# The list of all steps put in another order: packed attention and SwiGLU MLP on one core

## The chip, the cores and the metric

The kernel runs on one core of one Trainium2 chip. The metric is the device time of one execution in microseconds (us), as the median of several runs; a lower time is better. The engines of the core are called PE (TensorE), ACT (ScalarE), DVE (VectorE), POOL (GpSimd) and SP (SyncE, which here only issues transfers).

## The reference

Two stages follow each other. The attention takes q, k and v of 8 batches, 8 heads, 576 tokens and 64 elements, and p of 8 batches, 8 heads, 32 rows and 64 elements. The MLP takes the attention's output as 4608 tokens of 512 elements.

```python
packed = sm_attn(p, k, v)          # 32 rows per batch and head
out = sm_attn(q, packed, packed)   # softmax(q @ packed.T / 8) @ packed
x = out.transpose(0, 2, 1, 3).reshape(4608, 512)
xn = x / sqrt(mean(x * x, axis=-1) + 1e-06) * rms_g
g = xn @ w_gate                    # 512 x 1536
val = xn @ w_val                   # 512 x 1536
result = (g * 1 / (1 + exp(-g))) * val @ w_out   # 1536 x 512
```

## The kernel before

The 4608 tokens are cut into 12 units of 384 tokens (NU = 12), and the attention into 8 batches. The first attention, of p on k and v, is called stage 1 in the code and done batch by batch; the second attention, of q on the packed rows, and the MLP are done unit by unit. The product of a batch's packed rows with the gate and value weights is computed ahead ("packed weights", kept in buffers named ring), and the MLP's first product of a unit runs on it.

Every strand of work is a Python generator, called a chain: the keys, the loads of v, stage 1, the loads and conversions of the weights, the gram steps (which take scales from the weights), the queries, the attention of the units, the packed weights of the batches, and the MLP. A chain yields a step at a time and says on which engine the step runs. Each step issues a few instructions. `Plan.run` (L107 to L128) goes through the list `ORDER` (L129 to L181), two letters for a step, takes for each entry the chain of that number and issues its next step. Since every engine executes its instructions in the order in which they were issued, the list fixes the order on PE, ACT, DVE and POOL and the order in which SP issues transfers. No engine overtakes; which engine waits for which follows from the data and from the rooms (buffers) that chains take and give back. The list has 3289 entries, of which 903 are steps on PE, 903 on ACT, 830 on DVE, 427 on POOL and 226 on SP. A wait ahead of a step holds up all later steps of the same engine.

`FILLS` (L182 to L185) lists matmuls on dummy data (256 columns each, L1826) with the number of the PE step ahead of which they are put, how many of them and into which buffer they write.

The lines that matter in what follows: the gram steps are matmuls at L467, L472 and L517, with DVE at L470 to L478 and POOL at L482 to L489. Weights are converted by POOL (L410), DVE (L412) and ACT (L406). The packed weights are matmuls at L1074 and L1086, evicted by ACT at L371 and by DVE at L373. Stage 1 has its scores at L774, POOL's sum of two halves at L884 (behind a DMA transpose, L879) and its values at L915. The attention of a unit has its scores at L1327, the softmax on DVE at L1341 to L1351, transposes on PE at L1201 with copies by ACT at L1211, the values at L1398, a power step on POOL at L1444, a scaling of the result e on ACT at L1476, and the copies of the transposed result by ACT at L1225 and DVE at L1227. The MLP's gate and value products are at L1527, its SiLU on ACT at L1609, the product with it on DVE at L1612, and its last product at L1592, with a variant of seven products at L1723 for the later units.

Of the kernel before, what the change touches and what calls it, by code (L numbers as in the profile page):

```python
# [44 lines left out]
class Plan:  # L45
# [89 lines left out]
    "A9A-AZAZAZAfAeAcBAA5A+AeAdBAAVAfBAA+A6AfA1AbA6AYA5A4A4A5BAA5A5A5A6BBAeAZAZAeAdA5AfAUA6AfBCBBA1AVA6BCAZA6A6BCAfBB"
    "A6AgAYBBAgAZBEAgBEAZAZBDBDArA5BCBDA1BFA6A5ArA6AsBFBDBEAZACAZA6ACBEArACAsACAtACBGACBGAZAXACBFACAXBGAZAZAZBFAsBGAC"
    "ACBHACBIAWACACAZAXAtAYBHBIACAXAtAAAAAAAAAAAAAvBIAuAWAABHAZAZAZAZAZAZBHAZAZAuAXAWAAAXAAAZAZAXAuAZAvAXAYAXAXAZAWAA"
    "AwAYAZAZAwBJAXAvAABJAABJAXBJAZAZBIAXAwAXAXAWAZAZAZAZAAAXAXAWAXAXAWAWAWAZAZAZAZAZAZAXAWAXAZBKBLAWAAAXAYAAAAAXAABM"
    "AXBMAXAAAZBMAAAXAABMAZAZAZAXAABLBKAZAXAAAZAZAZAZAZAZAXAABNAZBOAZAXAYBOBPBPAYBOAZAXBPBOAABRAXBQBQAXBQAABQBRAZAZAZ"
    "AYBPBSBRAABSAAAAAYAXAZBRBUBTBTBUBTBSAXBSBTBUAZAZAYBUAZAZAXBVBVAYAXBWAXAXBVBWBWAZAZBXBXAXBWBYAABXAYBVBYBXACBYACAY"  # L140
    "BaBaBaAXBYAZAZBbAXACAZAZBaBbACAZAXAZACBcACBcBbAZAZBbBcBdAXAXAWBdAWBcBZBZACBeAXAZAXAWAZAXBeAWBdAXAZAXACBdAXAXAZAC"
    "AWBeACACACAZAAAAAAACAWAAAWAZAABeAZAZAZAZAZBNAZAZAZAXAZAZAAAWAZAZAAAZACACACACACAZAZACAZAZAAAAAAAWAAAZAAAWACBfAZAZ"
    "AABgAAAABfAWACBgACACACACACAZAAAAACACACAZAZACAAAZACAAAYAAAZACAAAXAZAZAYAZACAXAZAZAZAABhACAAAhBhBiAhAAAYAXBhAYAZBk"
    "AXAZAZBkBjBlBkBlBkAhAZAZAZBmBlAYAZBjAABhBmAAAYAXAhBlBmBnAXBjBnAZAZBmBjAYBoBoBoAABnBpAhAYBqAABpBnAXBqBqAZAZAZBqBr"
    "BoAhBpBrAZAZBiAAAXBrBpAYBsBrAhAZAZBuBsAXAXBuBsAXAXBuAXAXAZAZBsACAhBvBtAZAZAhBvAZBuBwBvACBvBxACAYBwAXAhBxByAhAYAC"
    "ACAhByAXAXAZAZBxAYAhACAWBwB0B0AZAWAXAXBtAWBwB0BxAWAXAZAZB0AZAZAZAZAWAZACBzAXBzAXAXAXAXAXBzACAhAWAZAZACACACACBzAC"
    "ACAAAAAAAAAhAWAXAZAZAZB1AZACACACAZAZAZAZAZAZAZAZAZAAAhAZAWAZAZAZB1ACAAAWAAAWAhACAhAWACAhAWAAAAAAB2AhByAAAZACACAC"
    "AAAhAhACACAhAZAZAZAZAZACB2AAACACACACAhACACByAhAAAXAYB3AZAhAXB3AZAZAZAZACAAB4AXB3AZAXAhB5AYAZB5AhACB7B5AhB5B7AkAh"
    "B3AhAXB6AZAZAZAZB7B6AkB8AhB8B7B9AhB9B8AhAAB8AZAZAZAZB-AhAXAhB-AAB6AhB-B9B-B9AZAZAAAhACAhCAB6CAAXB+AACAACAAB+CAAX"
    "AZAZAXAXAZB+CBAACBAAB+AZAXCBCCAXAZAZAZAXAXAAAhAACCCBCCAZAXAXAhAXAhCCAhCECDCEAXAhAZAXAXCEAACEAhAXAAAZAAAZCDAZAZAX"  # L150
    "AWB4AAAZCDCFAWAhCFCFCDAhCFAAAXAXAhAZAZAZAZAZAZAZAZAZAZAZAZAZAZACAXAhAZAXAhAWAXAXAhAWAhAWAZAZAZCHAWAWAWAWAWAXAZAZ"
    "AhACAZACACACAZAZAZAZAZAZAWAhACAhAhAhAhAhCHAXACCGAhAhACAhAXCIAZAZAZAZAhACACAhACAhACACAXAXAZAACGAAAZAZAAAZACCKAXAA"
    "CJAZAZCICKCKCLAXAhCLAXAYAZCKCNCMAhCLACCMAZCNAhCMAZCJAXCNCLCOCMAAAZAhAZAZCOACAhAXAXCNAXAXAXAAACAAAXAYAXCOCPAZAXCP"
    "AhCOAXCQACCQCQAACRCQAhAYCRAACSAhCSCPAZAZAZAhCSCPAhCTAACSAAAhAAAhAhCTCRACAZAZAZAlAAAYCUCVCUCUCUAlCTCWCRCTCVCWAZAZ"
    "CWAAAACWACCXACAAAACXAZAlAlAZAZAAAZCZCVCYACAAAXCYAAAACVCXCZAZAZACAZAZCYAWAACZCYCXAZACAXACAAAZAZAhCZAZAZAlAXAAAXAC"
    "ACACACAWAWAWAXAZAZAZAZAWCaAZAXAZACAXAXAWACCaAWACAlAXAlAZAZAWAWACAWAAACAlAAAmAmAmAZAZAYCbAYCcAAAmAmAmCcCbAAAZCcCb"
    "AXAWAZAZCcCbAlAZAZACAlAZAZAZAZAZAZAmAXAZAZAACdAmAXAmAmAXACAZAZAZACAZACAZAnAnAnAnAnCdAnACAZCfAXCgAZAZChAkAZAZAXCg"
    "ACAZChCiAZAXCiAYCgAnCiCjAnCgCkAkAYCfCeClCkCjCkClCiAZAZCjClCkAoChAZAZAoCmChAZAXCnCmACCmAnClCnACAZAkAkCnAYCoAnCoAo"
    "AoCpCnAXCpAXCpCoAoAoCmCoAZAZAXAZACCqACCjCqAZAZCpAXAXAoAkAZCrCrAXCrAoAZAZCsAXCqCsCsCtAXCtACACACACAAAZAZAZCrAAAWAX"
    "AZCuAZAXACAAAZCsCqAZAZAAAAAWAAAAACCuAAApApApAYACCeACAAACAWAAAAAZCuAXAZCtACAWCvAAAACtAZAZAWAoCuAWAXAoAWAXAWAWAZAZ"  # L160
    "AZAZAZAZAXCwAWAXAWACCvACAXAZAZAZAZApACAAAAAAAACwAAAXAZAZACAXAACvAWCvAAAXAZACACAZAZAZAAAXAZAZAZAZAAACACApAAACApAC"
    "ApACACACApACAYAAApApAXCxCyCyAqAZAZAZAZAZAZCyACAqAqAqAqAqAXAZAZAACxCyAkAXAACzAAC0AXAXAZAZAYAZAAC1AqC0C0AZAZAXC2C1"
    "C0AqC2AZC3ACC1ACAqC1C3C4C2C1C1C1C1C3C2C4AACzACAqAZAZC6C1C4C1C1C1ACAZAZC6C4C1ACC6C3C1C7C7C6C4AXC4C4ACC4ACC7ACAZC7"
    "C7C7AZAZAZC9C4C7ACC9C8AXC8C9C7C4AXC9C8C4C8AXAZAZC-C7C7AXC-C-C7C9AZAZAZC9C-C7C4AXC9C9C5ACACC4C+AXAXC4AXAXC+AXC7C+"
# [24 lines left out]
)
# [1692 lines left out]
```

## Time and profile before

| what | value |
| --- | --- |
| runs | 715.92, 718.26, 715.59 us |
| median | 715.92 us |
| profiled execution | 717.6 us, with a span of 715.8 us |
| PE busy in the span | 697.8 us (97%) |
| DVE, ACT, POOL busy | 515.4, 496.2, 350.1 us |
| instructions of PE | 8367 matmuls and as many weight loads |
| mean granted clock | 0.998 of 2.4 GHz |

The span goes from the first to the last instruction of one execution; the rest of its time lies outside. PE counts as busy from a matmul's start to its end. The matmuls overlap, so a mean duration of one is longer than the time that it adds. Idle time in brackets behind an instruction is time in which its engine did nothing ahead of it, with what ended that wait. A line of ACT, DVE or POOL with a wait is of interest only where PE comes to wait for it.

### The profile page before, as it was taken

What the parts mean: (1) busy time and instruction counts of PE and PEld (TensorE: products, weight loads), DVE (VectorE), ACT (ScalarE), POOL (GpSimd) and SP (SyncE); (2) the same over time, 40 slices, a digit from 0 to 9 for tenths busy, and PEclk for the clock granted to TensorE, in tenths of its full rate; (3) what the DMA queues carried; (4) which work ended last, traced back from release to release, by engine and by line L of the source; (5) the groups of instructions that cost most, each with busy time, mean ns of one, the idle gap of its engine ahead of it and who ended that gap; (6) DMA issues with size and microseconds to landing.
All of it is one profiled execution on the core that took longest, in us unless ns stands there. A gap on an engine that the chain in (4) does not pass through costs nothing.

```text
span 715.8 us, 20438 instructions
## 1 busy us (share of the span) xinstructions
PE 697.8 (97%) x8367; PEld 460.4 (64%) x8367; DVE 515.4 (72%) x1126; ACT 496.2 (69%) x1095; POOL 350.1 (49%) x468
## 2 busy tenths in 40 slices
...
GB/s 294 367 375 260 239 3 83 104 164 167 50 166 186 253 136 209 210 115 145 247 225 210 183 113 248 162 224 234 186 138 192 124 164 64 148 104 38 31 0 45
DMA packets 157103, 118.23 MB, mean 165 GB/s; under 512 B 117201, under 2 KB 140497, under 8 KB 153170
## 3 DMA queue, kind: packets, MB, share of 16 engines
...
q8 instruction: 65, 1.06, 0.6%
...
## 4 chain that ended last, share of the span: by engine, by line
PE 81%; DMA 6%; DVE 4%; ACT 4%; POOL 3%; issue 2%; SPq 1%; POOLq 0%; ACTq 0%; DVEq 0%
PE pm_1x L1527 9%; PE pm_3x L1527 9%; PE pm_0x L1527 8%; PE pm_2x L1527 8%; PE pm_3x L1592 8%; PE pm_2x L1592 7%; PE pm_0x L1592 5%; PE pm_1x L1723 3%; PE pm_0x L1723 3%; PE pm_3x L1723 3%; PE pm_2x L1723 2%; DMA ring<-in_moe_w_gate_dram 2%; PE psa L1086 1%; PE psb L915 1%; PE psa L1327 1%
## 5 line engine op out<-in xcount | busy, mean ns | idle before, releaser
L1527 PEld LDWEIGHTS <-ring 128*128 128x128 f16 x2304 | 204.7, 98 | 86.5 <-issue 14.9
L1592 PEld LDWEIGHTS <-hall 128*128 128x128 f16 x792 | 74.9, 98 | 89.0 <-issue 4.0
L1656 POOL TENSOR_TENSOR hall<-a_0x,hall 128x384 f16<-128x384 f32 (+1 forms) x36 | 32.5, 903 | 64.9 <-ACT hall L1653 64.8
L1637 POOL TENSOR_TENSOR hall<-t_1x,hall 128x384 f16<-128x384 f32 x32 | 32.7, 1021 | 59.3 <-ACT hall L1634 52.0
L1592 PE MATMUL pm_2x<-wo,hall 128*128 128x512 f16 x252 | 57.3, 379 | 0.0
L1592 PE MATMUL pm_3x<-wo,hall 128*128 128x512 f16 x252 | 56.8, 379 | 0.0
L1592 PE MATMUL pm_0x<-wo,hall 128*128 128x512 f16 x216 | 48.3, 379 | 0.0
L1527 PE MATMUL pm_0x<-aTu_0x,ring 128*128 128x384 f16 (+1 forms) x318 | 45.8, 287 | 1.2 <-DVE t_1x L1612 0.8
L1527 PE MATMUL pm_1x<-aTu_1x,ring 128*128 128x192 f16 (+1 forms) x336 | 47.0, 283 | 0.0
L1723 PEld LDWEIGHTS <-hall 128*128 128x128 f16 x432 | 41.9, 98 | 5.9
L1527 PE MATMUL pm_3x<-aTu_1x,ring 128*128 128x384 f16 (+1 forms) x306 | 44.6, 288 | 0.1
L1527 PE MATMUL pm_1x<-aTu_0x,ring 128*128 128x384 f16 (+1 forms) x300 | 43.5, 288 | 0.3 <-DVE ring L373 0.2
L1159 POOL TENSOR_TENSOR wgv<-o_0x,wgv 128x512 f16<-128x512 f32 x19 | 22.9, 1203 | 34.9 <-ACT wgv L1157 34.9
L1527 PE MATMUL pm_3x<-aTu_0x,ring 128*128 128x192 f16 (+1 forms) x276 | 39.0, 284 | 0.4 <-ACT t_1x L1609 0.3
L1527 PE MATMUL pm_2x<-aTu_1x,ring 128*128 128x384 f16 (+1 forms) x258 | 37.7, 289 | 0.7 <-ACT t_1x L1609 0.7
L1527 PE MATMUL pm_2x<-aTu_0x,ring 128*128 128x384 f16 (+1 forms) x258 | 36.7, 285 | 0.3 <-ACT t_1x L1609 0.3
L1527 PE MATMUL pm_0x<-aTu_1x,ring 128*128 128x192 f16 (+1 forms) x252 | 35.5, 284 | 0.0
L1637 POOL TENSOR_TENSOR hall<-t_0x,hall 128x384 f16<-128x384 f32 x24 | 23.9, 997 | 19.7 <-ACT hall L1634 18.3
L884 POOL TENSOR_TENSOR a1T_0x<-a_1x 96x768 f32<-96x768 f16 x9 | 15.1, 1676 | 37.0 <-DMA a_1x<-hl_0x 25.4
L373 DVE SCALAR_TENSOR_TENSOR ring<-psa,ring 128x512 f16<-128x512 f32 x30 | 20.6, 686 | 11.5 <-ACT ring L371 11.5
L371 ACT ACTIVATE ring<-psa 128x512 f16<-128x512 f32 x30 | 17.8, 593 | 13.5 <-DVE ring L373 6.7
L1653 ACT CAST hall<-a_0x 128x384 f16<-128x384 f32 (+1 forms) x36 | 17.6, 488 | 9.0 <-DVE a_0x L1612 8.5
...
## 6 DMA issues: line engine op xcount, KB each, us to landing
...
```

The source lines that it names most:

```text
L371: nc.scalar.activation(hi, x, AF.Copy, scale=s)
L373: nc.vector.scalar_tensor_tensor(lo, x, s, hi, ALU.mult, ALU.subtract)
L884: nc.gpsimd.tensor_tensor(a1T, x[:, 0], x[:, 1], ALU.add)
L915: nc.tensor.matmul(pp[32 * j : 32 * j + 32, :D], a1T[:, c, 32 * j : 32 * j + 32], vf[:, j, cv, :], start=(c == 0), stop=(c == NCK - 1),)
L1086: nc.tensor.matmul(ps[e][32 * j : 32 * j + 32, :], pg[h, lp, j, :], w16[h, j, lw, :], start=(n3 == 0), stop=(n3 == 2),)
L1159: nc.gpsimd.tensor_tensor(wgv16[:, c, k, 1], st, wgv16[:, c, k, 0], ALU.subtract)
L1527: nc.tensor.matmul(psi[:, :, o : o + n], pw[:, g, lw, w, f * P : (f + 1) * P], aT[:, :, la, g, o : o + n], start=(j == 0), stop=(j == 5),)
L1592: nc.tensor.matmul(po, hall[:, ft, lh, ts], wo[:, ft, 1 - lw, :], start=(n == 0), stop=(n == 3 * NFT - 1))
L1637: nc.gpsimd.tensor_tensor(hall[:, ft, 1, :], t, hall[:, ft, 0, :], ALU.subtract)
L1653: nc.scalar.copy(h3[:, 0, own], x3[:, own])
L1656: nc.gpsimd.tensor_tensor(h3[:, 1, own], x3[:, own], h3[:, 0, own], ALU.subtract)
L1723: nc.tensor.matmul(ps[:, :q], A[k](c, la), W[k](c, lw), start=(c + n3 == 0), stop=(c == NFC - 1 and n3 == 2))
```

## The change

Only the list `ORDER` and the list `FILLS` change. All functions, all buffers and all instructions on the data stay. The new list has the same 3289 entries in another order. Of the steps of each engine this many stay at the same place of their engine's order: 665 of 903 on PE, 286 of 903 on ACT, 255 of 830 on DVE, 185 of 427 on POOL, 117 of 226 on SP. The lists are text of letters; their first and last lines and the fillers are these:

```diff
 ORDER = (
-    "ABAAAAAAAAAAADAAAWAEAFAAAAAAAAAAAAAAAAADAAAAAAAAAAAAABAxADAxAyADAxADAEAyAWAWAxAxAxAxAGAHAWAxAyAEAxAEAFAxAFAFAyAW"
...
-    "AZAZEYAZEYEYAZEWAZAZAZAZAZEaAZAZAZAZAZEaAZEaAZEZEaEZAZAZAZAZAZAZEaEaEaEaAZEaAZEaEa"
+    "ABAAAAAAAAADAAAAAAADAAAAAAAAAAAAAAAAAAAAAWADAAAAAAADAxAEAWAxAWAFAxAxAyAEAxAyAxABAxAWAxAyAEAWAEAxAWAFAGAHAIAJAyAD"
...
+    "AZAZEYAZAZAZEYEYEYAZAZAZEZEaAZAZAZAZAZAZEaAZEaAZAZEaAZAZAZAZAZAZEaAZEaEaEZEaEaEaEa"
 )
 FILLS = (
-    (0, 29, "pm", 0), (1, 4, "pm", 0), (8, 5, "pa", -1), (20, 3, "psc", 0), (23, 1, "psc", 0),
-    (24, 5, "psc", 0), (28, 37, "pm", 0), (31, 6, "pm", 0),
+    (0, 29, "pm", 0), (5, 4, "psc", 0), (20, 3, "psc", 0), (21, 2, "psc", 0), (23, 3, "psc", 0),
+    (25, 6, "pm", 0), (28, 16, "pa", -1), (29, 12, "pm", 0), (35, 8, "pm", 0), (41, 2, "psc", 0),
+    (42, 4, "psc", 0),
 )
```

## Rows read from the trace of the kernel before

**Rows 1.** Part 1 of the page: busy us, share, instructions of each engine.

```profile
PE 697.8 (97%) x8367; PEld 460.4 (64%) x8367; DVE 515.4 (72%) x1126; ACT 496.2 (69%) x1095; POOL 350.1 (49%) x468
```

**Rows 2.** Chain that ended last: start us, length us, what, instructions.

```profile
165.32 7.77 PE pm_0x L1592 x36
```

**Rows 3.** Stretches: length; busy PE, PEld, DVE, ACT, POOL; clock, DMA share, GB/s.

```profile
0.00:53.70 53.70, 45.92 (x663) 35.52 (x663) 36.69 (x80) 31.80 (x59) 28.25 (x47) 0.97 1.01 345
53.70:80.00 26.30, 24.29 (x246) 15.24 (x238) 23.99 (x41) 21.86 (x38) 19.35 (x23) 1.00 0.76 261
...
490.00:712.60 222.60, 222.41 (x2399) 156.78 (x2396) 129.81 (x284) 123.80 (x309) 109.42 (x186) 1.00 0.40 105
```

**Rows 4.** Timeline of PE: start us, length us, engine, instruction, [idle before, releaser].

```profile
310.77 0.39 PE L1086 MATMUL pm_3x<-wgv,pgh_0x 64*32 64x512 f16 x1
...
313.26 0.37 PE L1086 MATMUL pm_3x<-wgv,pgh_0x 64*32 64x512 f16 x1 [2.10 <-issue]
```

**Rows 5.** Timeline of PE near 465 us, stage-1 values of batch 6.

```profile
465.57 0.88 PE L915 MATMUL psb<-big_4x,a1T_0x 96*32 96x64 f32 x48 [0.76 <-DMA big_4x<-in_v_dram]
```

**Rows 6.** Part 3 of the page: DMA queue, packets, MB, share of 16 engines.

```profile
q8 instruction: 65, 1.06, 0.6%
```

**Rows 7.** Timeline of DVE in the front.

```profile
40.43 1.22 DVE L412 SCALAR_TENSOR_TENSOR wgv<-wgv,hall 128x1024 uint32<-128x1024 uint32 x1
...
52.54 0.94 DVE L1227 SCALAR_TENSOR_TENSOR aTu_0x<-psa,aTu_0x 128x768 f16<-128x768 f32 x1
```

**Rows 8.** Timeline of ACT in the front.

```profile
42.07 0.71 ACT L371 ACTIVATE ring<-pm_3x,gv_r 128x512 f16<-128x512 f32 x1
...
45.62 1.35 ACT L1476 ACTIVATE e_0x<-e_0x,trio_3x 128x256 f32<-128x256 f32 x3
```

**Rows 9.** Timeline of POOL in the front.

```profile
39.08 1.22 POOL L482 TENSOR_SCALAR tiny_14x<-tiny_14x 128x2 f32<-128x2 f32 x1
...
40.70 1.09 POOL L484 TENSOR_SCALAR ratio<-tiny_14x,gv_r 128x1 f32<-128x1 f32 x1
42.75 0.88 POOL L1444 TENSOR_TENSOR trio_2x<-trio_1x,neghalf 128x3 f32<-128x3 f32 x1 [0.96 <-DVE trio_1x L1438]
...
46.63 0.27 POOL L484 TENSOR_SCALAR ratio<-tiny_16x,gv_r 128x1 f32<-128x1 f32 x1
```

**Rows 10.** Timeline of PE, first and last wait between 53.7 and 80 us.

```profile
65.09 1.14 PE L1527 MATMUL pm_0x<-aTu_0x,ring 128*128 128x384 f16 x6 [0.77 <-DVE t_1x L1612]
...
78.01 1.14 PE L1527 MATMUL pm_0x<-aTu_0x,ring 128*128 128x384 f16 x6 [0.45 <-ACT a1T_0x L867]
```

**Rows 11.** Timeline of PE: two batches' stage-1 scores (L774) and values (L915).

```profile
207.01 0.67 PE L774 MATMUL psa<-big_1x,pT_0x 128*32 128x288 f16 x16
...
221.36 0.88 PE L915 MATMUL psb<-big_5x,a1T_0x 96*32 96x64 f32 x48
...
222.06 0.68 PE L774 MATMUL psa<-big_3x,pT_0x 128*32 128x288 f16 x16
...
234.08 0.88 PE L915 MATMUL psb<-big_4x,a1T_0x 96*32 96x64 f32 x48 [0.24 <-POOL a1T_0x L884]
```

**Rows 12.** Timeline of POOL, its sum of the first of these batches.

```profile
218.67 1.63 POOL L884 TENSOR_TENSOR a1T_0x<-a_0x 96x768 f32<-96x768 f16 x1 [1.19 <-DMA a_0x<-hl_0x]
```

**Rows 13.** Timeline of PE, attention of the second unit.

```profile
102.06 0.85 PE L1201 MATMUL psb<-ident,e_0x 128*128 128x128 f32 x6 [0.26 <-DVE e_0x L1351]
...
105.80 0.27 PE L1398 MATMUL psa<-pk_0x,aT_0x 32*64 32x64 f32 x1
```

**Rows 14.** Timeline of ACT, attention of the second unit.

```profile
103.18 0.57 ACT L1211 ACTIVATE aT_0x<-psb 128x512 f32<-128x512 f32 x1
```

**Rows 15.** DMA issues: what, queue, kind, count, median us to landing.

```profile
a_1x<-hl_0x SPq DMA_TRANSPOSE x9, 4.5
...
big_3x<-big_1x SPq DMA_TRANSPOSE x1, 7.2
```

**Rows 16.** Waits of PE: instruction, releaser, us in all, times, longest.

```profile
PE pm_3x L1074 <- DVE ring L373: 2.5, 2, 2.0
```

More of the change, by code (lines that the diff above doesn't have):

```diff
@@ L135 @@
[L135 to L164, printed above, removed]
@@ new lines @@
+    "AyAKAWALAyAFAyAyAxAQAyAFAyACAQACAGAWACAQAQAXAGAxAHACAyAWAIAGAQAHAMAQAHAIACARAXAXAJAJAIAXAJAKARASAXACAXAXACAKACAK"
+    "ALASALAXAXAXAXARASARAYAXALATAXAXAQASARANATASATAXAYAzAzARAzATAMAYASAMAXAXAWAWAzAWATAXAWANAMAXAYAYAYA0A0AUAXAWANAX"
+    "A0A1ANAUA1A0ATAYAUA1AOAWAXAOA2APAXAUA1ARAYAUAOAPAOA3A3AaAAAAAAAAAAAAAPAZAVAAAZA4AUA3APAAAaAbA3AAAAA2AAAVAAAAAaA4"
+    "AaAZAVAAAAAaAcASAYAAAbAAAAAAAbAaAZAZA8AAAbA8AcAVAcAYA6AVA2AbAZATA9AdAcA4A9AdA4A-AbA8AeAdAZAZA-A8AZA-AeA+AdA2A9Ac"
+    "AdAZA6A-A+AZAVAeA9BABAAcBAAeA6AZA6A5AfAdA7A+A6A+AfAfA6BAA6AUAeA7AeAfA6AZA7A6AZA5A7BBAYAfBCA7BBBCA7AVAfA6AgA7AZAY"
@@ new lines @@
+    "AgAgA7A2BBAZBBBEBCBDBEBDBDAZA7BDAZAZA7ACArA7BCBFBEBEAsAZACArArACAXACBGBFBGA6BFA2AsBFACBGAZAZACAZBGAtAZACACAXACBH"
+    "ACACAZACAsBIACAXACBIAvAZAZAZAZAZAZAAAWAWAtAAAAAAAAAAAXAZAtAZAXAYBHAuBIAYAXAuAWAuAXAABHAXAWAAAwAAAXAXAXAWAAAXAZAX"
+    "AZAZBJAvBIAWAAAXBHAWAvAAAwBJAZAWAABJAWAXAZBJAZAZAwAZAXAXAYAAAAAXAZAZAWAZAZAZAZAXAZBKAAAYAAAZAXAXAXAZAZAWBKAAAXAA"
+    "BMAZAXAZAZAXAABLBMAZAZAXAABMAXAZBMAAAZAZAZAZAZAZAXAABNAZAXAYBOBPAXBOAZBOAXBPBOAYAAAZBRBQAXBPBQBPBQBQAXAABRAZAZAZ"
+    "AYAABSAYBRAXBRAABSAAAZBTBUAZBTBSAABVBVBNBTBUBTAZAZAXBUBSBWAXAXAYAZAXAXAXBUBWAYBXAXBXAZAZBWBYBYBWBYBYBZAYACBZAXAY"
@@ new lines @@
+    "AZAZACBXBZBaBXBaAZBaBaBbACBbAXACACAZBZBcACAZAZBcBbACBbBcBdAXAZAZBcAZAWAXAZAZBeACAZACAXAXBeAXAXAXAXBdAXACACACAAAA"
+    "AAAAAXAAAAACBdBeAABdAZAZAZAZAZAZACACAWACACBeACAZAZAAAWAAAZAZAZAZAZAAAWAAAWAAAWAAAWBfAWAZACAZAZAZAZAZAZAWAAAWACAZ"
+    "ACAZAAACACACAZACACBfBgAWAAAABLAZAZACAAAZACBgACACAAAYAAAAAZAAAXAZAXAYAZAZAABhAZAZAXBhAZAZBiACAYBhAXBjAZAYAXAhBjBj"
+    "AAAZAZAhACBjBlBlAXBkBlBkAZBmBmBhBlAYAhAZAZAhBnAAAYBmBnBkAZAAAAAZBmBkAYBoAYAABpBnBnBqBpBoACBpAZAZAZAXBrAhBoAhBqAA"
+    "BpBqACBrAYBqBiBrAZAZBrBtAXAZBuAZBoAhBtBuAZAZAhAXBtAZAXAXAXBuAXBtAXACAXBvAZAhBuBvBwBvAXBwAYAZACBwBvBwAhAhAYByACAX"
@@ new lines @@
+    "ByACACACBxAZAYBxAZAXAXAhAWBsBsBzAXB0AZAZAZBzB0AZAWACAhBzAZAZAZBzAXAXAXACAhAZACAXAXAXACB0ByAWBxAWByACACB0ACAWACAA"
+    "AAAAAAAZAZAZAZAXB1AAAhAZAZB1AZAZAZAZAZAZAZAZAZAZACACAWACAWAWAhAWACAAAhAWAAAAAWAhBxAZACAAAZACAhAAAAAhACACAWAZAZAh"
+    "AhACACACAZAZAZAZACAAAhACACAhACACAhACB2ACAhAXAAAZAZAZACACAXAhB2AZACAZAZACAAAAB3AXAYB4B3AXB5B4AhAYB4AZAhAZB5B7AZAZ"
+    "B4AhAXB7B5B8B7AZAZAXAhB5B6AhB8B7AAB9B6B8AhAhAZB8AZB9B6AhB-AAAhB-B-AhB-AZAZAZAZB9AhB9CAB+AhB6CACAAAAZAAB+AZAkAAAX"
+    "AZCAAhAAB+CBB+CBAXAAAXAXAZCCCBAZAZAXAXAAAXCBAXCCCCAXAXAhCCAhCDAZAZAZAXAhCEAXCDAXCEAAAhAZAZAZAZAZAXCEAXAhCEAAAZCD"
@@ new lines @@
+    "CFAhAACFAAAhAAAWAZCDCFAhAAAXAXAZAZAXAWAXCFAhAZAZAXAhAZAWAXAZAXAWAhAZAZAZAZAZAZACAZAWCHAWAWAZAZAZAWAWAWAXAZAZACAh"
+    "AhACACACAhACAZAZAhAhCHAhAWACCGCIAZAZAZAZAZAhAZAXAZAZAZAhACAhAhCIAXAXACAhAhAhACACACACACAkAAAXAhAZAZAZCKAZAZCJCKAA"
+    "AZAZAXAAAhCLAXAXAACKCLCLCKCJCMCMCMAhACAYCNAZAZCNCNCNAXAhCLAZAZCOAZAhACAXACAXAXAXACCMAACGAACOAXAXAYAAAhAXAZCPCOAh"
+    "COAXCPAYCQCQCQAACRCQCSCRAhAACPAXAhCSAAAZAhAZCPAZAhCSCTCSAAAhCTAZAZAAAZAhAhACAYAlCUCTCUAXCVCUCWCWAACVCRAZCWCWAZCT"
+    "AXACAlAAAAACCXAAAZAZCUAZCRCYACAACVACAZAAACAWCXAWCXCYAAAXAXCZACCZAACZAAACAhAlAZAZAZAlCXCVCYAXAXACAAAWAAAXAWAZAZCZ"
@@ new lines @@
+    "AZAXACAZACAXAWACCYAWAWACACAZAZAWAZAZAZAZAlAlAZAZACAZAAAWAWAlAlACAZAZAYAYAZAACbAZAZCcAACbAlAXAZAZAZAZAZCbCcAACaAZ"
+    "AZAZAWAACdCcCaAAAlAmCcACAXAZAZAmACAZAZCbAXAmAmAmCdAZAZACAmAkCeAZAkAZAXAmACAmCfAmACAZAZAZAXCgChAXCgAZAZAZCiAZChAX"
+    "CiCfACAXAYAYCeCiAnCgChAmCjCkCjAZAZChCkCkCkCgAZAZCjClClACCiAkAnAnCmAnACAnAnClCnClCnCmCjAnCnCnAZAZAZAXAnAZCmCpCoAX"
+    "ACAoACAnAZAZCoCqCmCpAZAZAnAXCoAZAXAXAXAXCqAXCpCrAoACAoCqACCpACCrAoACAYAkAAAAACCqAZCtAXCsCsCsCtAZCoAZAoAXAAAAAWAA"
+    "AACrAAAXAZCuAWAkAZAZACCuAACrAZACAAACCtAAAZAZAZAZAZAWAXAWCtCuACAAAWAAAYAoCuAoAZAZAZAZACAZAZAWAWAZAZAAAWACAoAWApAp"
```

54 lines of the change are left out of this document (27 added, 27 removed).

## The prediction

> **What bounds the kernel now.** I read the totals of the engines first: TensorE (PE) is busy for 697.8 of 715.8 us, and the next engine, VectorE, for 515.4 [rows 1]. Busy could still mean slow, so the second view is the chain of work that ended last. It has a run of 36 matmuls of the MLP's last product, of 512 columns each, in 7.77 us [rows 2], 216 ns each: at 2.4 GHz, the upper of the clock's two levels, which the granted clock of 1.00 in the third view means [rows 3], 512 columns take 213 ns. So PE is at its column rate there, and a new order cannot make that work shorter. The third view, the busy time of each engine by stretches, shows where there is anything to win. PE stands idle for 18.0 us in all [rows 1]: 7.78 before 53.7 us and 2.01 from there to 80 us, but only 0.19 in the 222.6 us from 490 to 712.6 [rows 3]. Of the rest, one wait of 2.10 us lies at 313.26 [rows 4], one of 0.76 at 465.57 [rows 5], and 3.2 us behind the last matmul (712.6 to 715.8) belong to the output's transfer. An order of steps can win only in those places, and can lose anywhere that it shortens the cover of a wait that PE does not see today.
>
> The sum is made against the profiled execution: a span of 715.8 and 1.8 outside it, 717.6 us. The runs gave 715.92, 718.26 and 715.59, so the profile is 1.7 above their median.
>
> **The change, part by part.** Decoding both lists step by step gives the same 3289 steps, and of PE's 903 steps 665 stand at the same place, none more than 10 places off. The other engines are shuffled more: 286 of ScalarE's (ACT) 903 steps, 255 of VectorE's (DVE) 830 and 185 of GpSimd's (POOL) 427 keep their place. Exponential and SiLU steps alternate on ACT 31 times in both lists, so the table loads stay. PE's order from 640 us of its work on is unchanged. The terms:
>
> *Filler matmuls, 90 to 89.* One of 256 columns at 216 ns for 512 is 0.11 us: -0.11, and their new places are at steps where PE waits anyway.
>
> *The wait at 313.26.* It stands between two matmuls of one and the same step (L1086, the first at 310.77 ran), and the profile finds no releaser [rows 4]. Nothing in the order asks for it. Without it the profiled time would be 715.5, which is where two of the three runs lie. I take -2.10; bounds 0 and -2.10.
> The 65 packets of the instruction queue hold 1.06 MB [rows 6], 16.3 KB each. The Trainium skill, "Runtime: NRT & Kernel Launch", section "Instruction fetch mechanics", says that each engine refills its instructions in blocks of 16 KiB and that a crossing is mostly hidden. The size agrees with the row. If it holds, the wait is no cost of each execution: the sum stays as below, and the rival in which the wait comes again has a smaller chance than the runs give it. No row shows that PE waited for its instructions there.
>
> *The front, up to 80 us.* Four steps change places in a way that matters. PE's first packed weights of batch 0 (L1074) now stand behind the second half of a gram (L467 to L472) that needs a weight conversion, and DVE ends that one (L412) at 41.65 [rows 7]. So the first eviction of ACT (L371), at 42.07 [rows 8], moves to about 43.5: +1.4. On POOL the power step of the attention (L1444), at 42.75, now stands behind a first gram step, a second one and a conversion. The first waits for two small steps of DVE that come behind the conversion ending at 41.65, so it starts near 42.0 and not at 39.08, and takes 2.7 as before (39.08 to 41.79); the conversion and the second gram step, which filled POOL from 43.63 to 46.90, take 3.3 [rows 9]. 42.0 + 2.7 + 3.3 gives 48.0 for the power step: +5.2. Queued behind it on ACT is the scaling of e (L1476), at 45.62 [rows 8], which goes to about 49; ACT has evictions and a conversion to do meanwhile, so it does not stand still for all of it. Behind that scaling come PE's transposes and their two evictions, of which DVE's (L1227) ended at 53.48 [rows 7], and for which the first MLP matmul waits. Placing these steps by hand with the durations of the rows gives DVE's end at 55.1: +1.65 for the first MLP matmul. Against this, three later gram steps of POOL (L487 to L489) are put off behind conversions, which come up to 1.4 us earlier, and PE's waits after 53.7, 2.01 us in all [rows 3], the first of them 0.77 at 65.09 [rows 10], have room to take up the delay. The 0.45 at 78.01 is set by a transfer of the last output weights and its conversion and stays [rows 10]. So 2.01 - 0.45 = 1.56 us absorb the 1.65: net +0.09; bounds -1.56 and +1.65.
>
> *A batch's stage-1 attention near 207 us.* Between its scores (end 207.68) and its values (221.36) lay 13.7 us of other PE work [rows 11]; in the new list it is 11.4. The chain from scores through exponential, DMA transpose and POOL's sum (L884) ended at 220.30 [rows 12], 12.6 us after the scores. The sister that follows, scores end 222.74 and values 234.08, got through in 11.3 us with a wait of 0.24 [rows 11]; the nearer row, since in the new list ACT's steps of this chain lie together in the same way. I take +0.5; bounds 0 and, with this batch's own 12.6 against 11.4 and a late landing on top, +2.
>
> *Stage-1 values of batch 6.* PE waited 0.76 at 465.57 for a load of v [rows 5]. In the new list these values come 4.7 us of PE work later, with the load at the same place: -0.76. The cover is other MLP matmuls; if the load moved too, the wait would stay: bounds -0.76 and 0.
>
> *Attention of the second unit.* The transposes of e wait 0.26 for DVE at 102.06; in the new list 1.1 us more work lies ahead of them: -0.26. They end at 102.91, ACT's copy (L1211) at 103.75, and the product that reads it (L1398) starts at 105.80 [rows 13, 14]. Now only one step of packed weights, about 1.0 us, lies between, where ACT needs 0.84 without a hand-over: +0.3; bounds 0 and +0.6.
>
> Other moved steps (loads of v for the last batch, a DMA transpose that stands behind a store on SP's queue, query transposes, weights streamed earlier) keep at least 2 us of cover, and I cost them at nothing. The cover is PE work of the MLP; DMA transposes land after 4.5 us in the median of one kind and after 7.2 in the slowest [rows 15], so a cover that is gone would cost up to 2.7.
>
> Sum: 717.6 - 0.11 - 2.10 + 0.09 + 0.5 - 0.76 - 0.26 + 0.3 = 715.3 us.
>
> **The rivals.** *The wait without a releaser comes again*: 715.3 + 2.1 = 717.4. For it: one of the three runs is 2.3 above the other two. Against: the median of three does not have it.
>
> *The front gets shorter (faster).* If POOL's put-off gram steps let the conversions and with them PE's weights come early, the delay of 1.65 does not occur, the 1.56 us of waits vanish, and the longest wait of the front, 2.0 us of L1074 for DVE's L373 [rows 16], goes too: 715.3 - 0.09 - 1.56 - 2.0 = 711.6. For it: the conversions on POOL do come earlier. Against: the power step is behind them.
>
> *ACT stands still behind the power step (slower).* ACT takes its steps in order. The scaling of e had 2.0 us of slack behind the power step (43.63 to 45.62) [rows 8, 9]. If POOL is over 2.0 late and ACT's evictions in between do not fill that, everything behind, evictions, PE's weights and the first MLP matmul, moves by the whole 5.2, and the later waits move with it, so they absorb nothing: 715.3 - 0.09 + 5.2 = 720.4. It decides from the point where ACT's work placed ahead of the scaling ends before POOL does. For it: 5.2 is more than twice the slack. Against: ACT has about 4 us of evictions and conversions there.
>
> *A shortened cover meets a slow transpose.* One of the stage-1 chains lands 2.7 us late [rows 15]: 715.3 + 2.7 - 0.5 = 717.5, and 720.2 if two do.
>
> *Nothing measurable is done*: the median stays at 715.9. The forecast's neighbour; the text cannot tell them apart.
>
> **How the numbers follow.** Forecast, with its neighbour: 0.46. Wait again: 0.14. Front shorter: 0.14. ACT stands still: 0.15. Slow transposes: 0.11, of which 0.04 end over 719.5. A measurement of this kernel can tell about 0.5%, 3.6 us, from no change: under 712.3 is faster, over 719.5 slower. So faster 0.14, slower 0.15 + 0.04 = 0.19, no change 0.67. The range reaches to the front's rival below, 711.2, and to the standing ACT above, 720.5; the forecast's own goes from 713.3 to 717.2.
>
> **What would show it.** Right: the first MLP matmul near 55.4 instead of 53.7; POOL's L1444 near 48; no wait of PE for the load of v at batch 6; PE idle from 490 us on still near 0.2; PE's busy time within 1 us of 697.8. Wrong: a wait of over 1 us of PE for L884 or L1211 in the middle; PE idle before 80 us under 7 or over 13 us; or a change of PE's busy time by more than 2 us, which no term here foresees.

## The result, and the profile after

The changed kernel takes 721.99 us (median of 5 runs, 721.59 to 724.09), the kernel before 716.68 us (5 runs). The ratio is 1.0066, with a 95% interval of 1.0041 to 1.0091. The forecast was 715.3, with a range of 711.2 to 720.5; the time lies 1.5 us above the range. The profiled execution took 721.99 us, with a span of 720.0.

The lines of the changed kernel are one higher than those of the kernel before (L688 is L687 there). First the totals and the stretches of the profile after, beside [rows 1] and [rows 3]. The columns of the stretches are length, busy time of PE, PE's weight loads, DVE, ACT and POOL, then granted clock, DMA share and GB/s.

```profile
PE 700.9 (97%) x8366; PEld 461.2 (64%) x8366; DVE 527.1 (73%) x1126; ACT 494.7 (69%) x1095; POOL 346.9 (48%) x468
```

```profile
0.00:53.70 53.70, 47.00 (x655) 35.56 (x663) 36.89 (x78) 30.88 (x59) 26.97 (x47) 0.97 0.99 333
53.70:80.00 26.30, 24.60 (x304) 15.89 (x284) 24.07 (x45) 22.82 (x39) 18.86 (x22) 1.00 0.96 315
...
320.00:460.00 140.00, 135.48 (x1475) 77.22 (x1473) 114.09 (x230) 105.06 (x236) 80.18 (x98) 0.99 0.79 186
...
490.00:716.00 226.00, 225.64 (x2439) 160.15 (x2437) 137.60 (x298) 127.56 (x322) 112.83 (x192) 1.00 0.41 112
```

Two things are to be seen. Between 320 and 460 us PE is idle for 4.5 us; in the kernel before it did not stand idle there at all:

```profile
320.00:460.00 140.00, 140.00 (x1582) 82.44 (x1581) 115.34 (x243) 108.94 (x241) 82.29 (x100) 1.00 0.81 190
```

And PE is busy for 700.9 us and not 697.8, with one matmul less. Of these 3.1 us, 2.0 lie at the place named next, where the clock was low, and 1.4 in the front; the other stretches take 0.3 off. The total alone says little: profiled once more (before_again), the kernel before was busy for 702.8 us.

The waits of PE name the place. It is the sum over the squares of k (L696) in the key preparation of batch 6:

```profile
PE psb L696 <- ACT big_4x L688: 4.5, 2, 3.9
```

```profile
399.19 0.16 PE L696 MATMUL psb<-tiny_71x,margin 96*128 96x2 bf16 x1 [3.86 <-ACT big_4x L688]
400.01 0.16 PE L696 MATMUL psb<-tiny_72x,margin 96*128 96x2 bf16 x1 [0.66 <-ACT big_4x L688]
```

The same matmul of the MLP can be found in both traces, and the difference of its start times says where time is won and lost. At each of these points PE has done the same matmuls in both, but for one filler:

| start in the profile before, us | 99.7 | 300.2 | 389.9 | 419.8 | 500.2 | 649.8 | 711.1 |
| --- | --- | --- | --- | --- | --- | --- | --- |
| after minus before, us | -0.51 | -1.37 | -2.13 | +4.37 | +3.58 | +4.13 | +4.12 |

The changed kernel is 2.1 us ahead when it comes to 390 us, and 4.4 us behind 30 us later: this one place costs 6.5 us. The two waits are 4.52 of them. The other 2.0 are for the most part the clock, as the stretches around the wait show:

```profile
395.00:399.20 4.20, 0.34 (x3) 0.11 (x2) 4.20 (x8) 1.00 (x3) 2.46 (x3) 1.00 0.17 62
399.20:403.00 3.80, 3.14 (x10) 1.22 (x10) 2.44 (x7) 3.52 (x8) 0.00 (x0) 0.63 1.04 199
403.00:407.00 4.00, 4.00 (x22) 2.03 (x21) 2.69 (x8) 2.21 (x6) 0.00 (x0) 0.93 0.55 106
```

PE had stood idle for 3.9 us, and the granted clock behind that is 0.63 in the mean, so for most of the time at the lower level of 1.2 GHz.

Now back along the wait, engine by engine. ACT has four steps L688, two for each of two buffers. The third of them waited 4.74 us for the third split of the query of unit 6 on DVE (L374, big_5x from big_4x): big_4x is the buffer into which q had been loaded, L688 writes its squares into the same buffer, and it comes free only when all three splits have read it. (The load of q itself was late for ACT's first step on it by 1.49 us.)

```profile
385.45 0.84 ACT L1279 ACTIVATE big_5x<-big_4x 128x768 bf16<-128x768 f32 x1 [1.49 <-DMA big_4x<-in_q_dram]
...
398.20 0.84 ACT L688 ACTIVATE big_4x<-big_2x 96x768 bf16<-96x768 f32 x1 [4.74 <-DVE big_5x L374]
```

DVE did not stand still. From its first split on it works without a gap, with the three splits at 388.82, 391.54 and 397.22:

```profile
388.82 0.75 DVE L374 SCALAR_TENSOR_TENSOR big_5x<-big_4x,tiny_69x,big_5x 128x512 f16<-128x512 f32 x1
389.49 2.13 DVE L1142 TENSOR_TENSOR wgv<-o_1x,wgv 128x512 f16<-128x512 f32 x1
391.54 2.76 DVE L374 SCALAR_TENSOR_TENSOR big_5x<-big_4x,tiny_69x,big_5x 128x512 f16<-128x512 f32 x1
394.23 1.21 DVE L1142 TENSOR_TENSOR wgv<-wgv 128x512 f16<-128x512 f32 x1
395.36 0.69 DVE L1469 TENSOR_SCALAR usc_0x<-gv_sc,tiny_62x 128x12 f32<-128x12 f32 x1
395.96 0.68 DVE L374 SCALAR_TENSOR_TENSOR ring<-pm_2x,ring 128x512 f16<-128x512 f32 x1
396.56 0.73 DVE L1801 TENSOR_SCALAR wgv<-pm_3x,invE 128x512 f32<-128x512 f32 x1
397.22 0.94 DVE L374 SCALAR_TENSOR_TENSOR big_5x<-big_4x,tiny_69x,big_5x 128x512 f16<-128x512 f32 x1
```

Two causes are in these rows.

The first is the order. Between the first and the third split stand five steps that are not the query's: two subtractions (L1142), a scale (L1469), an eviction (L374 into ring) and a store step (L1801). In the kernel before there were three. The subtractions belong to a chain that makes combinations of pieces of w_out for the seven products ("tee" in the code). POOL computes its additions and first subtractions (L1133, L1136), DVE the last ones. The new list runs this chain for piece 3 on POOL 7 to 13 us later than the old one did (the first addition starts at 369.8 and not 363.2, the last subtraction at 384.8 and not 372.0), so that both of its subtractions on DVE meet the query. POOL's additions for the next piece, at 382.1 in the kernel before, start at 391.03 and stand beside the splits.

The second is the length of four of the DVE rows. The same forms take 0.69, 0.75, 0.69 and 0.22 us in the kernel before where POOL stands still, 2.35 in all, and take 6.79 here. From the kernel before:

```profile
389.78 0.69 DVE L1141 TENSOR_TENSOR wgv<-o_0x,wgv 128x512 f16<-128x512 f32 x1
390.40 0.75 DVE L373 SCALAR_TENSOR_TENSOR big_1x<-big_3x,tiny_66x,big_1x 128x512 f16<-128x512 f32 x1
391.07 0.22 DVE L1468 TENSOR_SCALAR usc_0x<-gv_sc,tiny_58x 128x12 f32<-128x12 f32 x1
```

POOL's rows in the changed kernel at the time of the splits:

```profile
389.14 1.92 POOL L885 TENSOR_TENSOR a1T_0x<-a_1x 96x768 f32<-96x768 f16 x1 [0.53 <-DMA a_1x<-hl_0x]
391.03 1.60 POOL L1133 TENSOR_TENSOR o_0x<-wo 128x512 f32<-128x512 f16 x1
392.59 1.15 POOL L1133 TENSOR_TENSOR o_1x<-wo 128x512 f32<-128x512 f16 x1
393.72 1.17 POOL L1136 TENSOR_TENSOR o_0x<-o_0x 128x256 f32<-128x256 f32 x1
394.96 1.05 POOL L1136 TENSOR_TENSOR o_0x<-o_1x,o_0x 128x256 f32<-128x256 f32 x1
```

Each of DVE's two L1142 and its second split begins while one of these runs, and ends 0.55 to 0.56 us behind the end of one (391.62 behind 391.06, 394.30 behind 393.74, 395.44 behind 394.89), as if it began its work only then. The second split began at 391.54, ahead of POOL's second L1133 at 392.59, and still ended behind it: by these rows a DVE step that waits can be overtaken by POOL's next one. The eviction at 395.96 and the store step at 396.56, which read one operand from a PSUM tile (pm), keep their 0.68 and 0.73 although POOL is busy beside them.

The Trainium skill, "SBUF — State Buffer", section "Who interferes with whom", states that a DVE instruction with two inputs in SBUF contends with a GpSimd instruction that reads SBUF, and that one with at most one input there, outside the faster two-port modes, does not. The rows agree: L1142 and the splits have two, the eviction and the store step one at most. The scale L1469, with one tensor in SBUF, is longer beside POOL too (0.69 us and not 0.22); whether it ran in one of the excepted modes, no run here shows.

In the kernel before the same link was there with little to spare. The third split ended at 395.10, ACT's third L687 began at 395.12, and PE came to its sum at 397.30, 0.4 us after the last square was done:

```profile
393.88 1.22 DVE L373 SCALAR_TENSOR_TENSOR big_1x<-big_3x,tiny_66x,big_1x 128x512 f16<-128x512 f32 x1
...
395.12 0.84 ACT L687 ACTIVATE big_3x<-big_4x 96x768 bf16<-96x768 f32 x1
...
396.70 0.18 ACT L687 ACTIVATION_READ_ACCUMULATOR big_3x<-big_4x 96x1 f32 x1
...
397.30 0.17 PE L695 MATMUL psb<-tiny_71x,margin 96*128 96x2 bf16 x1
```

The new list moved the split's end to 398.16 (+3.1) and PE's arrival to 395.3 (-2.0). So about 2 us of the wait are the lead that PE had won before and loses here.

### The profile page after: what moved, and what is told of

Its sections match the earlier page's. It is cut to its first block, busy times and chain, and to the rows that moved or that the text cites. A ratio compares the mean times of both kernels' runs of the same rounds, so it can differ in the third digit from the quotient of the medians.

```text
span 720.0 us, 20445 instructions
## 1 busy us (share of the span) xinstructions
PE 700.9 (97%) x8366; PEld 461.2 (64%) x8366; DVE 527.1 (73%) x1126; ACT 494.7 (69%) x1095; POOL 346.9 (48%) x468
## 4 chain that ended last, share of the span: by engine, by line
PE 75%; DMA 9%; DVE 6%; ACT 5%; SPq 3%; issue 1%; POOL 0%; DVEq 0%; ACTq 0%; POOLq 0%
PE pm_1x L1528 8%; PE pm_0x L1528 8%; PE pm_2x L1528 8%; PE pm_3x L1528 8%; PE pm_1x L1593 8%; PE pm_0x L1593 7%; PE pm_3x L1724 3%; PE pm_3x L1593 3%; PE pm_2x L1724 3%; PE pm_0x L1724 3%; PE pm_2x L1593 3%; PE pm_1x L1724 2%; DMA hall<-in_moe_w_val_dram 2%; DMA ring<-in_moe_w_out_dram 2%; SPq L443 2%; DMA big_4x<-in_q_dram 2%
## 5 line engine op out<-in xcount | busy, mean ns | idle before, releaser
L1593 PE MATMUL pm_0x<-wo,hall 128*128 128x512 f16 x288 | 68.0, 386 | 0.0
L1593 PE MATMUL pm_1x<-wo,hall 128*128 128x512 f16 x252 | 56.1, 379 | 0.0
L1638 POOL TENSOR_TENSOR hall<-t_0x,hall 128x384 f16<-128x384 f32 x30 | 32.5, 1082 | 44.9 <-ACT hall L1635 42.0
L1528 PE MATMUL pm_3x<-aTu_1x,ring 128*128 128x192 f16 (+1 forms) x330 | 47.0, 286 | 0.0
L1528 PE MATMUL pm_1x<-aTu_0x,ring 128*128 128x192 f16 (+1 forms) x294 | 41.3, 284 | 0.1
L1528 PE MATMUL pm_1x<-aTu_1x,ring 128*128 128x384 f16 (+1 forms) x276 | 40.0, 288 | 0.7 <-ACT t_0x L1610 0.7
L1528 PE MATMUL pm_0x<-aTu_1x,ring 128*128 128x384 f16 (+1 forms) x276 | 40.0, 288 | 0.0
L1528 PE MATMUL pm_2x<-aTu_1x,ring 128*128 128x192 f16 (+1 forms) x270 | 37.9, 283 | 0.0
L885 POOL TENSOR_TENSOR a1T_0x<-a_1x 96x768 f32<-96x768 f16 x9 | 15.9, 1763 | 36.3 <-DMA a_1x<-hl_0x 36.2
L1593 PE MATMUL pm_3x<-wo,hall 128*128 128x512 f16 x144 | 32.2, 379 | 0.0
L374 DVE SCALAR_TENSOR_TENSOR ring<-psa,ring 128x512 f16<-128x512 f32 x30 | 20.5, 685 | 9.6 <-ACT ring L372 9.4
L1593 PE MATMUL pm_2x<-wo,hall 128*128 128x512 f16 x108 | 24.3, 379 | 0.0
```

The source lines that it names most:

```text
L374: nc.vector.scalar_tensor_tensor(lo, x, s, hi, ALU.mult, ALU.subtract)
L885: nc.gpsimd.tensor_tensor(a1T, x[:, 0], x[:, 1], ALU.add)
L1528: nc.tensor.matmul(psi[:, :, o : o + n], pw[:, g, lw, w, f * P : (f + 1) * P], aT[:, :, la, g, o : o + n], start=(j == 0), stop=(j == 5),)
L1593: nc.tensor.matmul(po, hall[:, ft, lh, ts], wo[:, ft, 1 - lw, :], start=(n == 0), stop=(n == 3 * NFT - 1))
L1638: nc.gpsimd.tensor_tensor(hall[:, ft, 1, :], t, hall[:, ft, 0, :], ALU.subtract)
```

## The experiments

The theory after the two traces: DVE's queue around the query's splits makes the wait, by order and by POOL's work beside it. Rivals: the load of q is late; PE comes too early for everything else. A diff of the list is shown as the steps that its letters stand for.

**The splits first (undo_dve).** On DVE the query's three splits stand together. This is more than the old order had, where three other steps stood between them.

```diff
 DVE  query of unit 6, split 1 (L374)
+DVE  query of unit 6, split 2; ACT and DVE: split 3
 DVE  tee 3, L1142
-DVE  query of unit 6, split 2
 DVE  tee 3, L1142; scale L1469; eviction L374; store L1801
-DVE  query of unit 6, split 3
```

> The changed kernel with one part undone: on DVE the second and third split of the query of unit 6 (L374, big_5x) stand again directly behind the first, ahead of the two tee additions (L1142), the scale (L1469), an eviction (L374) and a store step (L1801); ACT's half of the third split moves with them. Theory 'DVE queue': the buffer that ACT's L688 needs comes free with the third split, so it comes free at about 392 us instead of 398.2, L688 follows its first half at about 393.5, the wait of PE at L696 falls from 3.86 + 0.66 to under 0.8 in all, the clock stays at 1.00 and the time falls by about 6 us, to 716. Rival 'late load of q': the splits start at 388.8 as before and the third can only be as early as ACT's part; the wait would stay over 2 us if the load set it. Rival 'PE came too early': PE reaches L696 at 395.3 whatever DVE does, the time stays at 722.

Measured: 718.71 us (12 runs), ratio to the kernel before on the same chip 1.0022 (0.9996 to 1.0048), 3.3 us under the 722 of the changed kernel. The wait for the splits is gone, and behind it stands another one, of DVE's L924 (the eviction that frees a PSUM room), which still stood behind the store step:

```profile
401.58 0.18 PE L696 MATMUL psb<-tiny_71x,margin 96*128 96x2 bf16 x1 [2.24 <-DVE pk_1x L924]
```

The place costs 2.7 us (from +1.89 at 389.9 to +4.60 at 419.8) instead of 6.5. So what DVE's queue does ahead of the third split is a cause. The gain was half of what I expected, because the step that is late next stood in the same queue. POOL's work still lengthens the splits, which take 4.36 us for all three.

**The load of q earlier (q_load_first).**

```diff
 SP   load of q, unit 6, first half
+SP   load of q, unit 6, second half
 SP   loads of k, batch 6 (two)
-SP   load of q, unit 6, second half
```

> The changed kernel with the second half of the load of q for unit 6 issued on SP directly behind its first half, ahead of the two loads of k; nothing else moves. Rival 'late load of q': ACT's L1279 waited 1.49 us for this load and DVE 2.29 us for L1279, so the query's steps begin up to 2.3 us earlier, the wait of PE falls from 4.5 to about 2.2 us and the time by 2.3 us and half of the clock's share of 2.0, to about 718.5. Theory 'DVE queue': what stands ahead of the third split and lengthens it stays, so the gain is 1.5 us at most (the wait for the load), to about 720.5; and the loads of k, now later, may be late for L688.

Measured: 719.03 us, ratio 1.0007 (0.9983 to 1.0032). DVE now waits 0.69 us for L1279 and not 2.29, and the sum waits 1.82 us and 0.55:

```profile
384.71 0.16 DVE L1284 TENSOR_TENSOR tiny_64x<-tiny_64x,tiny_70x 128x1 f32<-128x1 f32 x1 [0.69 <-ACT big_5x L1279]
```

```profile
396.21 0.18 PE L696 MATMUL psb<-tiny_71x,margin 96*128 96x2 bf16 x1 [1.82 <-DVE pk_1x L924]
```

That is the rival's number: half of the wait goes when the load comes earlier, and the place costs 4.3 us (from -3.07 to +1.27). The load is a second cause, since DVE's queue begins with it.

**POOL's work beside DVE cut (pool_short).** The combination weights of one piece are left out but for 16 columns.

```diff
-            by.tensor_tensor(x, wo[:, f, 1, :], wo[:, f, 0, :], ALU.add)
+            w = 16 if i == 4 else DM
+            by.tensor_tensor(x[:, :w], wo[:, f, 1, :w], wo[:, f, 0, :w], ALU.add)
...
-            by.tensor_tensor(d, a, b, ALU.subtract)
+            w = 16 if i == 4 else q
+            by.tensor_tensor(d[:, :w], a[:, :w], b[:, :w], ALU.subtract)
```

> The changed kernel in which POOL's six additions and subtractions of the tee chain of w_out piece 4 (L1132, L1135) compute 16 columns instead of 512 or 256, so the combination weights of that piece are not made; order and all other steps stay. It tells POOL's share in the length of DVE's steps beside it. Theory 'POOL beside DVE': L1142, the second split, the second L1142 and L1469 took 2.13, 2.76, 1.21 and 0.69 us where the same forms took 0.69, 0.75, 0.69 and 0.22 in the kernel before; without POOL's work they fall back, the third split ends about 4 us earlier, at 394, the wait of PE falls under 1 us and the time to about 716.5. Theory 'order alone': DVE's steps keep their length, the time stays within 1 us of 722.

Measured: 716.63 us, ratio 0.9983 (0.9962 to 1.0004); the time is as expected. The order is that of the changed kernel, and DVE's rows are short wherever POOL's long work is gone (lines two higher than above):

```profile
389.58 2.13 DVE L1144 TENSOR_TENSOR wgv<-o_1x,wgv 128x512 f16<-128x512 f32 x1
391.64 0.74 DVE L374 SCALAR_TENSOR_TENSOR big_5x<-big_4x,tiny_69x,big_5x 128x512 f16<-128x512 f32 x1
392.30 0.70 DVE L1144 TENSOR_TENSOR wgv<-wgv 128x512 f16<-128x512 f32 x1
392.92 0.22 DVE L1471 TENSOR_SCALAR usc_0x<-gv_sc,tiny_62x 128x12 f32<-128x12 f32 x1
```

The first row keeps its 2.13, since POOL's L885 was left as it is and runs beside it. The third split starts at 394.31 and not 397.22, the wait at L696 falls from 4.5 to 1.4 us (I expected under 1), and the place costs 1.7 us instead of 6.5 (from -2.15 at 389.9 to -0.43 at 419.8). So POOL's work beside DVE is a cause, and the one whose removal gave most.

The three runs take 3.8, 2.2 and 4.8 us off the 6.5, together more than there is. Each of them brings forward the end of the same third split, so no share of the loss belongs to one cause alone.

**The clock alone (fill_wait).**

```diff
-    (42, 4, "psc", 0),
+    (42, 4, "psc", 0), (494, 34, "pm", 0),
```

> The changed kernel with 34 filler matmuls of 256 columns (0.11 us each, 3.7 us in all) put on PE ahead of L696, where it waited 3.86 us; nothing else moves. It prices the clock alone. If the fall of the granted clock to 0.63 behind the wait came from PE standing idle, the clock stays near 1.00, PE's matmuls of 512 columns behind the wait run at 216 ns again, and the time falls by about 2.0 us, to 720.0, with the wait itself still paid. If the clock falls for another reason, the time stays at 722. If the wait is shorter in most executions than in the profiled one, the fillers cost time instead, up to 3.7 us.

Measured: 721.52 us, ratio 1.0052 (1.0031 to 1.0072). In the profile the stretch behind the wait runs at a clock of 1.00, and the place costs 4.5 us (from -3.06 to +1.43), 2.0 less than without fillers:

```profile
398.70:402.50 3.80, 3.75 (x22) 1.93 (x22) 2.70 (x10) 3.24 (x7) 0.00 (x0) 1.00 1.09 209
```

So here PE's idling is what lowered the clock. The granted clock of whole executions agrees: 1.000 in ten of the twelve, and at most 0.998 in the twelve of the changed kernel run again. But such idling does not lower it each time: behind waits of 2.24 us in undo_dve and 3.57 us in before_then_after the clock stayed at 1.00, behind 2.37 us in q_load_first it was 0.68 in the mean of the next 3.8 us.

The medians show only 0.6 us of the 2.0 (722.15 to 721.52, not told apart). In the profiled execution 1.4 us are given back between 420 and 500 us, where the changed kernel gained 0.8, at two waits that it did not have (0.97 for ACT's L1687 at 432.36, 0.79 for a DMA transpose at 481.09). Where the gain goes in the other executions is not shown.

**All three moves (three_moves).** The two list edits above, and L916 and L924 ahead of the eviction and the store step (PE's own order stays as it is; on DVE L924 moves).

```diff
 DVE  tee 3, L1142; scale L1469
+PE and DVE: stage-1 values of batch 5 (L916, L924)
 DVE  eviction L374; store L1801
...
-PE and DVE: stage-1 values of batch 5 (L916, L924)
```

> The changed kernel with three parts moved around the long wait: the query's second and third split directly behind the first on DVE, the second half of the load of q ahead of the loads of k on SP, and the evicted stage-1 values of batch 5 (L916 on PE, L924 on DVE), for whose room PE waited 2.2 us in the run with the splits alone, ahead of the eviction and the store step on DVE. Theory 'DVE queue': nothing that PE's L696 needs is late any more, the wait at L696 is under 0.7 us, the clock stays, and the time is 6 us under the changed kernel's 722, at 716, some 1 to 2 us under the kernel before on the same chip. Rival 'PE came too early': a wait of 2 us stays with another releaser, and the time is 718.

Measured: 715.66 us (12 runs, 714.75 to 717.05), ratio 0.9971 (0.9951 to 0.9991): 6.3 us under the changed kernel's 721.99 and, as expected, some 2 us under the kernel before on the same chip. The three splits follow each other in 2.08 us, and L696 waits for nothing:

```profile
385.88 2.08 DVE L374 SCALAR_TENSOR_TENSOR big_5x<-big_4x,tiny_66x,big_5x 128x512 f16<-128x512 f32 x3
...
389.07 2.72 DVE L1469 TENSOR_SCALAR usc_0x<-gv_sc,tiny_62x 128x12 f32<-128x12 f32 x1
```

```profile
393.82 0.17 PE L696 MATMUL psb<-tiny_71x,margin 96*128 96x2 bf16 x1
```

POOL's work still lengthens a DVE row, now the scale L1469 (2.72 us for 12 columns), but nobody waits for that one.

**The lists cut and joined (before_then_after, after_then_before).** The remaining steps follow in the other list's order.

```diff
-ORDER of one list, 3289 steps
+the first 1480 (1500) steps of one list, then the other steps in the order of the other list
```

> The first 1480 steps (to about 336 us) in the order of the kernel before, with its fillers, the other 1809 in the order of the changed kernel. If the order of the steps from there on makes the long wait, PE waits 3 to 4.5 us at L696 near 400 us here too, and the time is 4 to 6 us over the kernel before. If the wait comes from the earlier part of the list (PE arriving 2 us earlier than DVE and the loads), it is under 1 us here and the time is within 1 us of the kernel before.

> The other way round: the first 1500 steps (to about 336 us) in the order of the changed kernel, with its fillers, the rest in the order of the kernel before. If the order from there on makes the wait, there is none over 0.8 us at the keys' L696 near 395 us, the wait of 0.76 us for the load of v near 465 us comes back, and what the front and the middle are worth is seen alone: 0 to 2 us under the kernel before, by what the trace of the changed kernel had gained by 300 us (1.4 us). If the early arrival of PE makes it, a wait of about 2 us stands at L696 and the time is 1 to 2 us over the kernel before.

Measured, the old front with the new rest: 726.8 us, ratio 1.0126 (1.0082 to 1.0170), 9.0 us over the kernel before where I expected 4 to 6. The wait is there (2.91 and 0.66 us), with PE as late as in the kernel before (0.5 us later at 389.9), so it does not need PE's early arrival:

```profile
400.88 0.16 PE L695 MATMUL psb<-tiny_71x,margin 96*128 96x2 bf16 x1 [2.91 <-ACT big_4x L687]
```

```profile
399.89 0.84 ACT L687 ACTIVATE big_4x<-big_0x 96x768 bf16<-96x768 f32 x1 [4.73 <-DVE big_3x L373]
```

The profiled execution took 721.89, the fastest of six, at a granted clock of 0.998; the others, up to 731.95, had 0.984 to 0.992. What lowered it there is not shown.

The new front with the old rest: 719.78 us, ratio 1.0029 (1.0009 to 1.0048). There is no wait at L696, and the one for v is back (1.18 us at 468.17), as expected. But PE is 2.2 us later at 389.9 than in the kernel before, so the run does not try this order with an early PE. The gain of the front is not seen in the time, which is 2.0 us over the kernel before: a new wait of 3.58 us stands close behind the joint, for a query's DMA transpose that was issued at 343.06 us:

```profile
349.85 1.35 PE L1328 MATMUL psa<-pbd,big_0x 128*128 128x64 f16 x22 [3.58 <-DMA big_0x<-big_5x]
```

**The two kernels once more (before_again, after_again).** No edit.

> The kernel before, unchanged, profiled once more. If the wait of 2.10 us at 313.26 without a releaser belongs to one execution and not to the order, it is not at the same instruction this time; a wait of that kind may stand elsewhere. If it belongs to the order, L1086 waits there again for 2 us. The front tells how far two executions of one order differ: the changed kernel and its three variants have so far reached the first MLP matmul within a span of 5 us.

> The changed kernel, unchanged, beside the kernel before on one chip. The wait of PE at L696 comes from the order of the steps, so it is there again, 3 to 4.5 us, with the clock down behind it, and the time is 3 to 6 us over the kernel before. If it came from loads that were late in one execution, it is under 1.5 us and the time within 2 us of the kernel before.

The changed kernel: 722.15 us, ratio 1.0057 (1.0037 to 1.0076), 4.0 us over the kernel before on the same chip. The wait is at the same place (4.04 and 0.66 us), which costs 7.3 us here (from -3.00 at 389.9 to +4.27 at 419.8):

```profile
398.61 0.16 PE L696 MATMUL psb<-tiny_71x,margin 96*128 96x2 bf16 x1 [4.04 <-ACT big_4x L688]
```

The kernel before: 718.84 us, ratio to itself 1.0018 (0.9997 to 1.0039). Its wait without a releaser stood ahead of the same instruction again, so it belongs to the order and not to one execution; its length does not repeat (1.16 us and not 2.10):

```profile
315.77 0.37 PE L1086 MATMUL pm_3x<-wgv,pgh_0x 64*32 64x512 f16 x1 [1.16 <-issue]
```

**Four fillers less (four_fillers_less).**

```diff
-    (0, 29, "pm", 0), (1, 4, "pm", 0), (8, 5, "pa", -1), (20, 3, "psc", 0), (23, 1, "psc", 0),
+    (0, 25, "pm", 0), (1, 4, "pm", 0), (8, 5, "pa", -1), (20, 3, "psc", 0), (23, 1, "psc", 0),
```

> The kernel before with the first group of fillers cut from 29 to 25, nothing else. In three executions of its list the wait without a releaser stood ahead of the same matmul, number 3794 of PE, in the middle of a step (L1086). Theory 'instruction fetch': the place is given by the count of PE's instructions, so with four matmuls fewer ahead it moves four matmuls on in the work (still number 3794, four later in the same 24 of L1086), 0 to 2.1 us long. Rival 'the data of this step': it stays ahead of the third matmul of those 24, now number 3790. Time within 1 us of the kernel before by both.

Measured: 718.74 us, ratio 1.0004 (0.9981 to 1.0027). The wait moved four matmuls on: six of the 24 ran ahead of it, where two did in [rows 4].

```profile
317.24 0.39 PE L1086 MATMUL pm_3x<-wgv,pgh_0x 64*32 64x512 f16 x1
...
318.28 0.37 PE L1086 MATMUL pm_3x<-wgv,pgh_0x 64*32 64x512 f16 x1 [0.64 <-issue]
```

It goes by the count of PE's instructions, not by the step.

## Why the prediction was wrong, point by point

- *The step that failed* is the paragraph on "other moved steps", which "keep at least 2 us of cover", costed at nothing. One moved group had 0.4 us of cover. I had looked at loads and transposes, whose waits have a transfer as their end, and not at a buffer that passes from one strand to another: the query's load buffer to the squares of k. No row of waits of PE in the kernel before showed that link, since nobody waited there. The place costs 6.5 us; 715.3 + 6.5 is 721.8.
- *The second fault, of the same step*: I took the durations of the rows as fixed. Where a step is moved beside another engine's work its duration moves too: 2.35 us of DVE work became 6.79.
- *The clock* was no term at all. The 4.5 us of idling cost another 2.0. My sign of PE's busy time within 1 us of 697.8 could not tell it either: the kernel before itself came to 702.8 when it was profiled again.
- *Front*: +0.09 forecast; -0.51 measured at 99.7 us. The steps were mis-sized: POOL's power step started at 44.48 and not 48, ACT's scaling at 48.50, the first MLP matmul at 54.09 and not 55.4. But no single profile can settle a term of this size there: undo_dve, three_moves and the changed kernel have the same front, and they came to the matmul of 53.8 us at +3.85, -1.03 and +0.34. The old list does the same: before_again came there at +3.79. In undo_dve PE waited 1.96 us for a load of v at 23.41, and the clock was 0.50 for the next 10 us; in three_moves it was 1.00:

```profile
25.00:35.00 10.00, 10.00 (x62) 9.29 (x62) 6.11 (x9) 4.94 (x10) 6.28 (x7) 0.50 1.05 387
```

```profile
25.00:35.00 10.00, 8.27 (x86) 7.22 (x85) 8.43 (x12) 5.50 (x8) 6.04 (x7) 1.00 1.04 383
```

- *The wait at 313.26*: -2.10 was right for the changed kernel, and the reason was wrong. The wait does not come and go with the execution, it belongs to the old list (2.10, 1.16, 1.11 and 0.64 us in the four profiled executions that begin with it, none there in the eight that begin with the new one). In its neighbourhood the new list has two waits that I did not foresee, in each of its profiles:

```profile
311.21 1.15 PE L1528 MATMUL pm_0x<-aTu_0x,ring 128*128 128x192 f16 x12 [0.86 <-ACT t_0x L1610]
...
313.84 1.15 PE L1528 MATMUL pm_2x<-aTu_0x,ring 128*128 128x192 f16 x12 [0.49 <-DVE ring L374]
```

- *Attention of the second unit*: right in size. The wait of 0.26 is gone, and 0.18 stands at the values (forecast +0.3), though for DVE's copy (L1215) and not for ACT's.
- *Stage-1 attention near 207 us*: +0.5 forecast, no wait measured; inside the bounds.
- *Values of batch 6*: right. The wait of 0.76 is gone, and the changed kernel gains 0.79 between 419.8 and 500.2 us. From there to 649.8 it loses 0.55 in small pieces, which no term had and whose cause is not shown.
- *The rivals*: none was the one that happened. "ACT stands still behind the power step" had the right sign and the wrong place. The range's ends, 711.2 and 720.5, were meant to be two rivals' times, which the prediction itself puts at 711.6 and 720.4.
- *Luck*: the sum up to 390 us was -1.6 by my terms and is -2.1. By stretches it was not that good: -0.51 and not -0.02 (fillers and front) up to 99.7 us, -0.86 and not +0.54 from there to 300.2, -0.76 and not -2.10 from there to 389.9. These misses of up to 1.4 us nearly cancel, so that 721.8 comes close to the measured 721.99. None of them is as large as the 6.5 us that was not listed.
